# Whole fp32 products for five pieces of the second weight in the first two token groups

## The chip, the cores and the metric

The kernel runs on one core of one Trainium2 chip. The metric is the device time of one execution in microseconds (us). Three runs of the kernel before took 847.70, 844.62 and 848.91 us, median 847.7. The core's engines are named as in the profile: PE is the matrix engine (PEld its weight loads), DVE the vector engine, ACT the scalar engine, POOL the general engine and SP the engine that issues most of the transfers.

## The reference, cut to what matters

Three layers follow each other. A gated linear recurrence over 768 positions (4 batches, 8 heads, head size 48) gives 3072 rows of 384 numbers. A dense layer computes h = x @ w_in (384 to 2048), g = h * sigmoid(h), and x2 = g @ w_out (2048 to 384). A routed layer then picks one of eight experts for each row.

```python
def _moe_ref(x, w_in, w_out):
    h = x @ w_in
    g = h * (1.0 / (1.0 + np.exp(-h)))
    return (g @ w_out).astype(np.float32)
```

The change concerns only the last line, g @ w_out, for the first four chunks of 128 rows.

## The kernel before, in words

The 3072 rows are 24 chunks of 128 rows. The chunks are taken in groups: two groups of two chunks (0 and 1), then groups of three, and a last one of two. The recurrence of a chunk runs in six stages (`att0` to `att5`); the last one leaves the transposed rows of the chunk, split into two parts, in `xth` and `xtl` (`big` for group 0).

Both weights of the dense layer are cut into 16 pieces. `in_0` to `in_15` are 128 columns of w_in, `out_0` to `out_15` are 128 rows of w_out (128 x 384). A weight arrives as 64-bit floats. `load_piece` fetches a piece as raw words into one of four buffers `raw`, and `narrow` makes 32-bit floats of it on DVE with three instructions (L295, L298, L301; the first also appears as L199) in one of two buffers `cv`. `split` then makes two parts of it: ACT writes the rounded part `hi` (L226) and DVE the rest `lo` (L227). Four pieces share a pair of tiles, so `out_0_lo` in a row stands for pieces 0 to 3 and `out_1_lo` for pieces 4 to 7.

For a group g and a piece i the dense layer runs three functions. `moe_h` makes nine products on PE into `ph` (three parts of the rows by hi and lo of `in_i`), ACT takes the tanh (`se`, L501) and DVE forms the gated value (`sg`, L503). `moe_g` splits this value: ACT writes `gh` (L511), DVE writes `gl` (L512). `moe_o`, two steps later, adds three products for each chunk to `px`: gh by out_lo, gl by out_hi, gh by out_hi. They use the rounded type fp32r, in which one pass over the columns makes a product. With two chunks this makes six products of 128x384 for one pair (g, i) in groups 0 and 1.

The order of work is a list `seq` of steps (g, i). The first six steps belong to group 0, the next six to group 1, then the two groups take turns until piece 15, and group 2 follows at step 32. Tables (`UI`, `UO`, `ST0` to `ST6`) say in which step a piece is loaded and a stage of the recurrence is run. PE keeps the order in which the program is written. For DVE, ACT and the transfer queue of SP the framework chooses an order when the kernel is built, by its own estimate of times; only a few instructions are pinned. On the chip every engine then works through its list in order and waits at the first instruction whose input is missing.

Plain fp32 products already exist in this kernel: `pl` of chunks 0 to 6 multiplies the constant triangle by the plain values `f` (128 x 384). A plain product shows in the trace as two MATMUL records.

The eight transfers `xs<-big` (776 KB each) fill a table in memory with zeros. Each waits for a small POOL instruction that reads the `lo` part of one of the pieces 12 to 15, so that it starts only when that piece has been split, and POOL also waits for the transfer before.

Of the kernel before, what the change touches and what calls it, by code (L numbers as in the profile page):

```python
# [9 lines left out]
F32 = mybir.dt.float32  # L10
# [3 lines left out]
U32 = mybir.dt.uint32  # L14
I64 = mybir.dt.int64
# [6 lines left out]
P = 128  # L22
CAP = 512
ROW = 388
# [32 lines left out]
SG = 2  # L57
SE = 2
GB = 3
# [22 lines left out]
LMIN = -43.9  # L82
GROW = math.exp(20.0 - LMIN)
PLAIN = 7
ST = ST0, ST1, ST2, ST3, ST4, ST5, ST6
FAR = float(1 << 20)
HEAD = 2
# [6 lines left out]
def kernel(  # L94
# [14 lines left out]
    nc = tc.nc  # L109
    B, H, S, D = q.shape  # L110
    NT, DM = out.shape
    DFF = moe_w_in.shape[1]
    E, _, F2 = moe2_w1.shape
# [7 lines left out]
    GT = CPG * P  # L121
# [14 lines left out]
    raw = main.enter_context(tc.tile_pool(name="raw", bufs=4))  # L136
    phase = ExitStack()
    att = phase.enter_context(tc.tile_pool(name="att", bufs=1))
    late = phase.enter_context(tc.tile_pool(name="late", bufs=1))

    def bank(kind, name):
        return ps.tile([P, 512], F32, tag=kind, name=name, bufs={"h": 2, "x": 3, "a": 3}[kind])
# [25 lines left out]
    def use(n, i, name):  # L168
        return bank(BANKS.get(n, "aaaaaaaa")[i], name)
# [28 lines left out]
    def keep(fn):  # L198
        return lambda *a, **k: tc.keep_in_program_order(fn(*a, **k))  # L199

    def new_unit(key):
        kind = key[0]
        full = [P, 4, KC, P] if kind in ("in", "w1") else [P, 4, DM]
        nm = "_".join(str(x) for x in key)
        units[key] = tuple(wts.tile(full, F32R, tag="wt", name=f"{nm}_{x}") for x in ("hi", "lo"))

    def part_of(src, kind, i, n):
        cols = slice(i * P, (i + n) * P)
        return (src[:, cols] if kind in ("in", "w1") else src[cols, :]).rearrange("(c p) f -> p c f", p=P)
# [14 lines left out]
    def split(key, h, x, lo_engine):  # L224
        hi, lo = units[key]
        (keep(nc.scalar.copy) if key == ("w1", 1, 1) and RT > 1 else nc.scalar.copy)(hi[:, h], x)  # L226
        lo_engine.tensor_sub(lo[:, h], x, hi[:, h].bitcast(F32))  # L227

    def load_piece(kind, i):
        u, h = divmod(i, 4)  # L230
        src = moe_w_in if kind == "in" else moe_w_out
        nm = f"{kind}_{i}"
        if h == 0:
            new_unit((kind, u))
        shape = [P, KC, P] if kind == "in" else [P, 1, DM]
        if src.dtype == I64:
            t = raw.tile(shape + [2], U32, tag="raw", name=f"{nm}_raw")
            made = len(pieces_made)
            pieces_made.append(i)
            load_raw(t.rearrange("p c f w -> p c (f w)"), src, kind, i, nc.scalar if made < RAW else nc.sync)  # L240
            x = raw.tile([P, ROW], U32, tag="cv", name=f"{nm}_cv", bufs=2)[:, :DM].rearrange("p (c f) -> p c f", c=shape[1])
            t2 = t.rearrange("p c f w -> p (c f) w")
            pin = keep if i < (PI if kind == "in" else PO) else lambda fn: fn
            narrow(t2, x.rearrange("p c f -> p (c f)"), pin)
            x = x.bitcast(F32)
        else:
            x = raw.tile(shape, F32, tag="raw", name=f"{nm}_raw")
            nc.sync.dma_start(out=x, in_=part_of(src, kind, i, 1))
        split((kind, u), h, x if kind == "in" else x[:, 0], nc.vector)

    def verify_piece(kind, i, s):
        src = moe_w_in if kind == "in" else moe_w_out
# [59 lines left out]
    def att0(n):  # L312
        f = loaded.pop(("f", n))
        g, _ = group_of[n]
        if g < 2 or n == starts[g]:
# [3 lines left out]
            nc.scalar.activation(t, t, AF.Ln, bias=1.0)  # L319
        if n < PLAIN:  # L320
            lf[n] = (f.rearrange("p h d -> p (h d)"),)
# [19 lines left out]
    def att1(n):  # L341
        pl = use(n, 0, f"pl_{n}")
        if n < PLAIN:
            pe.matmul(pl[:, :DM], tri, lf.pop(n)[0], start=True, stop=True)
# [142 lines left out]
    gt = {}  # L487
    ht = {}

    def moe_h(g, i):  # L490
        GT = sizes[g] * P
        xh, xl = (x[:, : sizes[g]] for x in xt[g])
        wh, wl = units["in", i // 4]
        ph = bank("h", f"ph_{g}_{i}")
        m = i % 4
        for c in range(KC):
            pe.matmul(ph[:, :GT], wh[:, m, c, :], xl[:, :, c, :], start=c == 0, stop=False)
            pe.matmul(ph[:, :GT], wl[:, m, c, :], xh[:, :, c, :], start=False, stop=False)
            pe.matmul(ph[:, :GT], wh[:, m, c, :], xh[:, :, c, :], start=False, stop=c == KC - 1)
        e = att.tile([P, GT], F32, tag="se", name=f"se_{g}_{i}", bufs=SE)  # L500
        nc.scalar.activation(e, ph[:, :GT], AF.Tanh, scale=0.5)  # L501
        t = att.tile([P, GT], F32, tag="sg", name=f"sg_{g}_{i}", bufs=SG)
        nc.vector.scalar_tensor_tensor(out=t, in0=e, scalar=1.0, in1=ph[:, :GT], op0=ALU.add, op1=ALU.mult)  # L503
        ht[g, i] = t

    def moe_g(g, i):
        GT = sizes[g] * P
        t = ht.pop((g, i))
        hi = att.tile([P, GT], F32R, tag="gh", name=f"gh_{g}_{i}", bufs=GB)
        lo = att.tile([P, GT], F32R, tag="gl", name=f"gl_{g}_{i}", bufs=GB)  # L510
        (nc.scalar.copy if g < GACT else nc.vector.tensor_copy)(hi, t)  # L511
        (nc.gpsimd if (g, i) < LOV else nc.vector).tensor_sub(lo, t, hi.bitcast(F32))  # L512
        gt[g, i] = (hi, lo)

    def moe_o(g, i):
        hi, lo = gt.pop((g, i))
        first, last = (0,), (NF - 1,)
        wh, wl = units["out", i // 4]
        if i in first:
            px[g] = [bank("a" if (g, t) == (1, 1) else "x", f"px_{g}_{t}") for t in range(sizes[g])]  # L520
        for t in range(sizes[g]):
            o = px[g][t][:, :DM]
            m = slice(t * P, (t + 1) * P)
            pe.matmul(o, hi[:, m], wl[:, i % 4, :], start=i in first, stop=False)
            pe.matmul(o, lo[:, m], wh[:, i % 4, :], start=False, stop=False)
            pe.matmul(o, hi[:, m], wh[:, i % 4, :], start=False, stop=i in last)
        if i in last:
            moe_x2(g, i)

    x2 = {}  # L530
# [575 lines left out]
    def at(slot, fn, *args):  # L1106
        plan.setdefault(slot, []).append((fn, args))
# [4 lines left out]
    for n in range(NCH):  # L1112
        g, r = group_of[n]
        if n < len(ST):
            so = ST[n]
            s0 = ld = LD[n]
# [15 lines left out]
    for u in range(4):  # L1132
        for h in range(4):
            at(UI[4 * u + h], load_piece, "in", 4 * u + h)
            at(UO[4 * u + h], load_piece, "out", 4 * u + h)
    for j in range(2 * NF):
        s = VS + j * VD // 2
        at(s, verify_piece, ("in", "out")[j % 2], j // 2, s)
# [54 lines left out]
    first = min(plan)  # L1193
# [15 lines left out]
    g = NG - 1  # L1209
# [8 lines left out]
    def preload():  # L1218
        for j in range(2):
            load_expert_unit(("w1", 1, j), nc.vector)  # L1220

    todo = dict(
        o=lambda: moe_o(*outs.pop(0)), f=lambda: fill(1), F=lambda: fill(len(ops)), l=lambda: logits_pe(g),
        m=lambda: logits_pe2(g), p=lambda: pick(g), r=lambda: route(g), w=preload, k=rank_rest,
        g=rest_fetch, t=lambda: turn(items["rest"]),
# [50 lines left out]
```

## Time and profile before

| what | value |
|---|---|
| median of three runs | 847.7 us |
| profiled execution: its own time | 845.27 us |
| profiled execution: span from first to last instruction | 843.6 us |
| PE busy | 810.5 us, 96% of the span |
| DVE busy | 483.4 us, 57% |
| ACT busy | 377.1 us, 45% |
| mean granted clock of PE | 0.989 |

The shares are averages over the whole span. In the slices of 21 us that the profile shows, DVE has 9 tenths in the second to the fifth slice and 4 to 6 tenths later, so the shares of the first 110 us are not those of the whole. A wait in the lists names the instruction that waited and the one that released it.

### The profile page before, as it was taken

How to read it: one execution, taken by the hardware profiler on the slowest of the kernel's cores; microseconds unless marked ns; L12 is line 12 of the kernel's file. 1: busy time of each engine (PE TensorE's matmuls, PEld its weight loads, DVE VectorE, ACT ScalarE, POOL GpSimd, SP SyncE). 2: the span in 40 equal slices, each digit the busy share in tenths (PEclk: the TensorE clock that was granted, in tenths of full speed). 3: DMA queues.
4: the chain of work that ended last, by engine and by line, in shares of the span. 5: the costliest groups of instructions: out<-in, count | busy, mean ns of one | idle time of the engine just before them, and what ended most of it. 6: DMA issues, size and time to landing. Idle time of an engine off the chain costs nothing.

```text
span 843.6 us, 15324 instructions
## 1 busy us (share of the span) xinstructions
PE 810.5 (96%) x5692; PEld 766.8 (91%) x5692; DVE 483.4 (57%) x1293; ACT 377.1 (45%) x805; POOL 59.1 (7%) x94
## 2 busy tenths in 40 slices
PE   7799989999999999999999999999999999999994
PEld 4689889999999999999999999989999999999993
DVE  5999965566665556555666556366464526435520
ACT  4565464453453453444444333365273525435520
POOL 2000000002001001001001000001110010110001
PEclk9899999999999999999999999999999999999998
DMA  9856863313244343254343321342281615624500
GB/s 206 189 147 163 250 193 96 66 39 101 74 100 104 74 94 106 67 105 104 76 95 94 86 57 48 104 132 67 97 276 55 200 56 171 200 80 164 168 16 27
DMA packets 166435, 95.92 MB, mean 114 GB/s; under 512 B 115692, under 2 KB 159965, under 8 KB 166352
## 3 DMA queue, kind: packets, MB, share of 16 engines
q1 hardware_dynamic: 162224, 83.80, 37.5%
q0 software_dynamic: 3280, 9.49, 2.9%
q10 hardware_dynamic: 848, 1.57, 0.6%
q8 instruction: 46, 0.75, 0.4%
q14 instruction: 37, 0.30, 0.1%
HBM read 75.61 MB, written 16.33 MB: 109 GB/s over the span
## 4 chain that ended last, share of the span: by engine, by line
PE 60%; DMA 12%; issue 10%; DVE 9%; ACT 4%; SPq 3%; POOLq 0%; POOL 0%; DVEq 0%; ACTq 0%
PE px L333 19%; PE ph L333 18%; DMA out_dram<-o,oi 6%; PE py L333 4%; PE po L333 4%; PE p L333 4%; PE sc L333 2%; DMA w_raw<-in_moe_w_dram 1%; DMA f<-in_f_logit_dram 1%; DVE am L404 1%; PE pl L333 1%; PE p_r L333 1%; PE po_r L333 1%; PE pq L338 1%; PE pk L338 1%
## 5 line engine op out<-in xcount | busy, mean ns | idle before, releaser
L333 PE MATMUL px<-out_lo,gh 128*128 128x384 f32 x384 | 137.3, 357 | 0.3 <-ACT gh L511 0.3
L501 ACT ACTIVATE se<-ph 128x384 f32<-128x384 f32 (+1 forms) x144 | 65.3, 454 | 159.7 <-PE ph L333 157.1
L333 PE MATMUL px<-out_hi,gl 128*128 128x384 f32 x384 | 130.2, 339 | 2.2 <-DVE gl L512 2.2
L333 PE MATMUL px<-out_hi,gh 128*128 128x384 f32 x384 | 129.7, 338 | 0.0
L333 PE MATMUL ph<-xtl,in_hi 128*128 128x384 f32 (+1 forms) x384 | 125.5, 327 | 1.2 <-DVE sg L503 0.9
L503 DVE SCALAR_TENSOR_TENSOR sg<-se,ph 128x384 f32<-128x384 f32 (+1 forms) x144 | 73.0, 507 | 90.9 <-ACT se L501 89.0
L333 PE MATMUL ph<-xth,in_hi 128*128 128x384 f32 (+1 forms) x384 | 124.0, 323 | 0.0
L333 PE MATMUL ph<-xth,in_lo 128*128 128x384 f32 (+1 forms) x384 | 123.8, 322 | 0.0
L511 ACT CAST gh<-sg 128x384 fp32r<-128x384 f32 (+1 forms) x144 | 68.7, 477 | 70.5 <-DVE sg L503 61.5
L512 DVE TENSOR_TENSOR gl<-sg,gh 128x384 fp32r<-128x384 f32 (+1 forms) x144 | 73.4, 510 | 29.2 <-ACT gh L511 28.1
L333 PEld LDWEIGHTS ph<-xtl,in_hi 128*128 128x128 f32 x384 | 72.5, 189 | 3.8 <-issue 1.4
L333 PEld LDWEIGHTS px<-out_hi,gl 128*128 128x128 f32 x384 | 72.6, 189 | 3.6 <-DVE gl L512 3.2
L333 PEld LDWEIGHTS px<-out_lo,gh 128*128 128x128 f32 x384 | 72.4, 188 | 3.2 <-ACT gh L511 0.9
L333 PEld LDWEIGHTS ph<-xth,in_lo 128*128 128x128 f32 x384 | 72.5, 189 | 0.0
L333 PEld LDWEIGHTS ph<-xth,in_hi 128*128 128x128 f32 x384 | 72.4, 189 | 0.0
L333 PEld LDWEIGHTS px<-out_hi,gh 128*128 128x128 f32 x384 | 72.3, 188 | 0.0
L227 DVE TENSOR_TENSOR w_lo<-w_raw,w_hi 128x384 fp32r<-128x384 f32 x128 | 65.1, 552 | 12.5 <-ACT w_hi L226 11.8
L333 PE MATMUL po<-w_lo,hh 128*128 128x384 f32 (+6 forms) x200 | 67.8, 339 | 0.0
L333 PE MATMUL po<-w_hi,hh 128*128 128x384 f32 (+6 forms) x200 | 67.2, 336 | 0.0
L333 PE MATMUL po<-w_hi,hl 128*128 128x384 f32 (+6 forms) x200 | 67.2, 336 | 0.0
L226 ACT CAST w_hi<-w_raw 128x384 fp32r<-128x384 f32 x124 | 56.9, 513 | 22.8 <-DMA w_raw<-in_moe_w_dram 19.5
L333 PE MATMUL p<-xsl,w_hi 128*128 128x480 f32 (+6 forms) x168 | 58.5, 348 | 0.0
(243 smaller groups left out, 1437.9 us busy)
## 6 DMA issues: line engine op xcount, KB each, us to landing
w_raw<-in_moe_w_dram SPq DMA_DIRECT2D x64, 384.0 KB
xs<-big SPq DMA_DIRECT2D x8, 776.0 KB
out_again<-in_moe_w_out_dram SPq DMA_DIRECT2D x16, 384.0 KB
xe<-xs SPq DMA_DIRECT2D x7, 776.0 KB
out_raw<-in_moe_w_out_dram SPq DMA_DIRECT2D x13, 384.0 KB
f<-in_f_logit_dram SPq DMA_DIRECT2D x24, 192.0 KB
k<-in_k_dram SPq DMA_DIRECT2D x24, 192.0 KB
q<-in_q_dram SPq DMA_DIRECT2D x24, 192.0 KB
```

The lines of the kernel that those rows point to most:

```text
L226: (keep(nc.scalar.copy) if key == ("w1", 1, 1) and RT > 1 else nc.scalar.copy)(hi[:, h], x)
L227: lo_engine.tensor_sub(lo[:, h], x, hi[:, h].bitcast(F32))
L333: ins = nc.tensor.matmul(*a, **k)
L338: ins = nc.tensor.transpose(*a, **k)
L404: nc.vector.tensor_tensor(out=a, in0=sc4, in1=tri4, op=ALU.mult)
L501: nc.scalar.activation(e, ph[:, :GT], AF.Tanh, scale=0.5)
L503: nc.vector.scalar_tensor_tensor(out=t, in0=e, scalar=1.0, in1=ph[:, :GT], op0=ALU.add, op1=ALU.mult)
L511: (nc.scalar.copy if g < GACT else nc.vector.tensor_copy)(hi, t)
L512: (nc.gpsimd if (g, i) < LOV else nc.vector).tensor_sub(lo, t, hi.bitcast(F32))
```

## The change

Pieces 0 to 4 of w_out are no longer split when they are loaded. `narrow` writes them into a tile of their own (`out_0_x` to `out_4_x`, in the five buffers that later hold the rows `x2`). For groups 0 and 1 the gated value of these pieces stays one plain tile (`sgp`, in a buffer of `gh`), and one plain fp32 product for each chunk takes the place of three. The split into hi and lo, which groups 2 and later use, is asked for in steps 28 to 33.

```diff
+SPL = 28, 29, 30, 31, 33
...
+            if whole(kind, i):
+                x = whole_home(i)
+            else:
+                x = raw.tile([P, ROW], U32, tag="cv", name=f"{nm}_cv", bufs=2)
...
+        if whole(kind, i):
+            wholes[i] = x[:, 0]
+        else:
+            split((kind, u), h, x if kind == "in" else x[:, 0], nc.vector)
...
+    def whole(kind, i):
+        return kind == "out" and i < len(SPL) and moe_w_out.dtype == I64
...
+    def whole_home(i):
+        return att.tile([P, ROW], U32, tag="x2", name=f"out_{i}_x", bufs=5)
...
+    def split_late(i):
+        u, h = divmod(i, 4)
+        split(("out", u), h, wholes.pop(i), nc.vector)
...
+        if g < 2 and whole("out", i):
+            t = att.tile([P, GT], F32, tag="gh", name=f"sgp_{g}_{i}", bufs=GB)
...
     def moe_g(g, i):
...
+        if g < 2 and whole("out", i):
+            gt[g, i] = t, None
+            return
...
+            if lo is None:
+                pe.matmul(o, hi[:, m], wholes[i], start=i in first, stop=i in last)
+                continue
...
+    for i, s in enumerate(SPL):
+        if whole("out", i):
+            at(s, split_late, i)
```

On PE nothing else moves: at ten places six products become two. DVE's list is rebuilt. The first place is DVE between the state update of chunk 0 and the last part of the rows of chunk 1 (`big<-pt_1`), which the first product of the dense layer needs. The last rows of this place in the kernel before:

```order
L462 TENSOR_TENSOR state_85<-pu_1_395,state_85 48x4x48 x2
L227 TENSOR_TENSOR out_0_lo_214<-out_2_cv_278,out_0_hi_213 128x384
L463 TENSOR_TENSOR state_85<-state_85,a_all_84 48x4x48 x2
L227 TENSOR_TENSOR in_0_lo_266<-in_1_cv_316,in_0_hi_265 128x384
L199 TENSOR_SCALAR out_3_cv_324<-out_3_raw_322 128x384
L199 TENSOR_SCALAR in_2_cv_351<-in_2_raw_348 128x384
L298 SCALAR_TENSOR_TENSOR out_3_cv_324<-out_3_raw_322,out_3_cv_324 128x384
L482 TENSOR_TENSOR big_91<-pt_1_461,big_91 128x384
```

The same place in the changed kernel:

```order
L228 TENSOR_TENSOR in_0_lo_262<-in_1_cv_310,in_0_hi_261 128x384
L200 TENSOR_SCALAR out_3_x_318<-out_3_raw_316 128x384
L482 TENSOR_TENSOR state_85<-pu_1_387,state_85 48x4x48 x2
L228 TENSOR_TENSOR in_0_lo_262<-in_2_cv_343,in_0_hi_261 128x384
L318 SCALAR_TENSOR_TENSOR out_3_x_318<-out_3_raw_316,out_3_x_318 128x384
L483 TENSOR_TENSOR state_85<-state_85,a_all_84 48x4x48 x2
L200 TENSOR_SCALAR in_4_cv_413<-in_4_raw_410 128x384
L321 SCALAR_TENSOR_TENSOR out_3_x_318<-out_3_raw_316,out_3_x_318 128x384
L502 TENSOR_TENSOR big_91<-pt_1_453,big_91 128x384
```

The splits of the pieces `out` are gone from here, and passes over pieces that stood behind `big<-pt_1` (all of `in_2`, the first of `in_4`, the last of `out_3`) now stand ahead of it.

The second place is DVE behind the masked scores of chunk 5 (`am_5_0`, `am_5_1`), up to the inputs of chunk 6 (`kpad0<-en_6`). In the kernel before it begins with these rows:

```order
L404 TENSOR_TENSOR am_5_1_1265<-sc_5_1_1254,trir_78 128x512
L298 SCALAR_TENSOR_TENSOR out_11_cv_1156<-out_11_raw_1154,out_11_cv_1156 128x384
L512 TENSOR_TENSOR gl_0_8_1293<-sg_0_8_1251,gh_0_8_1292 128x256
L295 TENSOR_SCALAR in_13_cv_1189<-in_13_raw_1186 128x384
L301 SCALAR_TENSOR_TENSOR out_11_cv_1156<-out_11_raw_1154,out_11_cv_1156 128x384
L298 SCALAR_TENSOR_TENSOR in_13_cv_1189<-in_13_raw_1186,in_13_cv_1189 128x384
L301 SCALAR_TENSOR_TENSOR in_13_cv_1189<-in_13_raw_1186,in_13_cv_1189 128x384
L227 TENSOR_TENSOR out_2_lo_895<-out_11_cv_1156,out_2_hi_894 128x384
L295 TENSOR_SCALAR out_12_cv_1223<-out_12_raw_1221 128x384
```

In the changed kernel it begins with these:

```order
L424 TENSOR_TENSOR am_5_1_1175<-sc_5_1_1164,trir_78 128x512
L538 TENSOR_TENSOR gl_0_8_1203<-sg_0_8_1161,gh_0_8_1202 128x256
L321 SCALAR_TENSOR_TENSOR in_14_cv_1196<-in_14_raw_1193,in_14_cv_1196 128x384
L228 TENSOR_TENSOR out_3_lo_1130<-out_12_cv_1133,out_3_hi_1129 128x384
L228 TENSOR_TENSOR out_0_lo_214<-out_0_x_217,out_0_hi_213 128x384
L228 TENSOR_TENSOR out_0_lo_214<-out_1_x_240,out_0_hi_213 128x384
L228 TENSOR_TENSOR out_0_lo_214<-out_2_x_274,out_0_hi_213 128x384
L228 TENSOR_TENSOR out_0_lo_214<-out_3_x_318,out_0_hi_213 128x384
L315 TENSOR_SCALAR out_13_cv_1239<-out_13_raw_1237 128x384
```

The pieces out_11, in_13 and nearly all of out_12 and in_14 are now ahead of am_5, and four of the five late splits have been placed behind it by the framework, well before the steps that the table names. The split of the fifth, out_4, stays early, between pieces 7 of `in` and 6 of `out`.

The third place is the transfer queue of SP, where the last pieces, the zero fill and the inputs `f` of chunks 7 to 9 meet. Before:

```order
L219 DMA out_15_raw_1482<-in_moe_w_out_dram 128x768
L1172 DMA xs_76<-big_91 128x4x388
L193 DMA f_7_1621<-in_f_logit_dram 128x8x48 x3
L358 DMA ends_75<-ep_6_1318 1x384
L193 DMA k_7_1627<-in_k_dram 128x8x48
L193 DMA q_7_1625<-in_q_dram 128x8x48
L1172 DMA xs_76<-big_91 128x4x388
```

Now:

```order
L220 DMA out_15_raw_1392<-in_moe_w_out_dram 128x768
L1204 DMA xs_76<-big_91 128x4x388
L194 DMA v_6_1031<-in_v_dram 128x8x48
L1204 DMA xs_76<-big_91 128x4x388
L194 DMA f_7_1531<-in_f_logit_dram 128x8x48 x2
L378 DMA ends_75<-ep_6_1228 1x384
L194 DMA f_7_1531<-in_f_logit_dram 128x8x48
```

The third zero fill now stands ahead of `f_7`, which waited behind two of them before.

## Rows read from the trace of the kernel before

**Rows 1.** Busy time of the engines in four stretches, with PE's clock and DMA share.

```profile
core 0: us, PE busy (x) PEld busy (x) DVE busy (x) ACT busy (x) POOL busy (x), PEclk, DMA share, GB/s
27.20:44.70 17.50, 14.71 (x121) 13.03 (x121) 15.87 (x37) 13.07 (x24) 0.00 (x0) 0.81 0.90 198
44.70:91.00 46.30, 44.68 (x369) 42.39 (x367) 44.58 (x111) 25.83 (x63) 0.00 (x0) 1.00 0.60 155
91.00:107.00 16.00, 12.73 (x83) 11.83 (x79) 15.86 (x38) 6.70 (x18) 0.69 (x3) 0.89 0.92 271
...
120.00:500.00 380.00, 378.53 (x2877) 362.28 (x2875) 223.07 (x619) 167.20 (x334) 16.54 (x19) 1.00 0.36 88
```

**Rows 2.** What PE waited for in the first 180 us: total, times, longest.

```profile
PE py L333 <- DVE state L460: 2.1, 1, 2.1
PE ph L333 <- DVE big L482: 1.5, 1, 1.5
```

**Rows 3.** Chain of work that ended last: start, duration to the next piece, what.

```profile
28.06 1.03 PE pq L338 x4
...
75.52 0.65 PE pl L333 x2
76.16 1.05 PE px L333 x6
...
80.72 0.44 PE pq L338 x4
```

**Rows 4.** PE in order of time: start, duration, instruction, [idle before and releaser].

```profile
32.71 0.39 PE L333 MATMUL ph<-big,in_hi 128*128 128x256 f32 x1 [1.52 <-DVE big L482]
...
47.28 0.39 PE L333 MATMUL ph<-big,in_hi 128*128 128x256 f32 x1 [1.03 <-ACT in_hi L226]
...
47.92 0.39 PE L333 MATMUL ph<-big,in_lo 128*128 128x256 f32 x1 [0.26 <-DVE in_lo L227]
...
89.96 1.16 PE L333 MATMUL sc<-qt,kt 48*128 48x128 f32 x16
```

**Rows 5.** DVE in order of time, 23 to 33 us.

```profile
23.43 0.74 DVE L460 TENSOR_TENSOR state<-pu,a_all 48x192 f32<-48x192 f32 x2
...
31.51 0.55 DVE L298 SCALAR_TENSOR_TENSOR out_cv<-out_raw,out_cv 128x384 uint32<-128x384 uint32 x1
32.09 0.56 DVE L482 TENSOR_TENSOR big<-pt,big 128x384 fp32r<-128x384 f32 x1
```

**Rows 6.** DVE in order of time, 91 to 109 us.

```profile
91.62 1.28 DVE L404 TENSOR_TENSOR am<-sc,trir 128x512 f32<-128x512 f32 x2
92.81 0.55 DVE L298 SCALAR_TENSOR_TENSOR out_cv<-out_raw,out_cv 128x384 uint32<-128x384 uint32 x1
93.28 0.42 DVE L512 TENSOR_TENSOR gl<-sg,gh 128x256 fp32r<-128x256 f32 x1
93.62 0.35 DVE L295 TENSOR_SCALAR in_cv<-in_raw 128x384 uint32<-128x384 uint32 x1
93.89 0.55 DVE L301 SCALAR_TENSOR_TENSOR out_cv<-out_raw,out_cv 128x384 uint32<-128x384 uint32 x1
...
103.63 0.55 DVE L354 SCALAR_TENSOR_TENSOR kpad<-en,k 128x384 f32<-128x384 f32 x1
...
108.11 0.75 DVE L317 TENSOR_SCALAR f<-f 128x1152 f32<-128x1152 f32 x1
```

**Rows 7.** SP's transfer queue and POOL in order of time, 100 to 106 us.

```profile
100.04 0.40 SPq L1172 DMA_DIRECT2D xs<-big  x1
100.53 4.86 SPq L193 DMA_DIRECT2D f<-in_f_logit_dram  x3
...
105.87 0.19 POOL L1170 TENSOR_TENSOR big<-in_lo 128x1 fp32r<-128x1 f32 x1 [5.86 <-DMA xs<-big]
```

**Rows 8.** ACT in order of time, 110 to 113 us.

```profile
110.68 0.38 ACT L501 ACTIVATE se<-ph 128x256 f32<-128x256 f32 x1
111.07 1.28 ACT L319 ACT_TABLE_LOAD   x1
```

More of the change, by code (lines that the diff above doesn't have):

```diff
@@ L240, in load_piece @@
             load_raw(t.rearrange("p c f w -> p c (f w)"), src, kind, i, nc.scalar if made < RAW else nc.sync)
-            x = raw.tile([P, ROW], U32, tag="cv", name=f"{nm}_cv", bufs=2)[:, :DM].rearrange("p (c f) -> p c f", c=shape[1])
+            if whole(kind, i):
+                x = whole_home(i)
+            else:
+                x = raw.tile([P, ROW], U32, tag="cv", name=f"{nm}_cv", bufs=2)
+            x = x[:, :DM].rearrange("p (c f) -> p c f", c=shape[1])
             t2 = t.rearrange("p c f w -> p (c f) w")
@@ L248, in load_piece @@
             nc.sync.dma_start(out=x, in_=part_of(src, kind, i, 1))
-        split((kind, u), h, x if kind == "in" else x[:, 0], nc.vector)
+        if whole(kind, i):
+            wholes[i] = x[:, 0]
+        else:
+            split((kind, u), h, x if kind == "in" else x[:, 0], nc.vector)
+    wholes = {}
+    def whole(kind, i):
[5 more added lines that the diff above has]
+        split(("out", u), h, wholes.pop(i), nc.vector)
     def verify_piece(kind, i, s):
@@ L501, in moe_h @@
         nc.scalar.activation(e, ph[:, :GT], AF.Tanh, scale=0.5)
-        t = att.tile([P, GT], F32, tag="sg", name=f"sg_{g}_{i}", bufs=SG)
+        if g < 2 and whole("out", i):
+            t = att.tile([P, GT], F32, tag="gh", name=f"sgp_{g}_{i}", bufs=GB)
+        else:
+            t = att.tile([P, GT], F32, tag="sg", name=f"sg_{g}_{i}", bufs=SG)
         nc.vector.scalar_tensor_tensor(out=t, in0=e, scalar=1.0, in1=ph[:, :GT], op0=ALU.add, op1=ALU.mult)
```

## The prediction

> **What bounds the kernel now.** I read four views, in this order. The table of busy time by stretch comes first, because the page's shares are means over very different stages. From 120 us on PE is busy 378.5 of 380 us [rows 1]: whatever delay or gain exists when the kernel gets there is carried to the end unchanged, so the whole question lies in the first 117 us. Up to there DVE is as full as PE: 15.9 of 17.5 us, 44.6 of 46.3 us and 15.9 of 16.0 us in the three stretches from 27 to 107 us [rows 1]. In the middle one PE is full too (44.7 of 46.3), in the other two it is not. The list of PE's waits then says for whom: almost always DVE, 2.1 us for the first state update, 1.5 us for the second part of `big` [rows 2]; a wait of 1.03 us for piece in_3 [rows 4] goes through ACT, which itself waited for DVE's passes. The chain of waits gives what one step costs on the path, and the clock: PE was granted 0.81 and 0.89 of full speed in the first and third stretch [rows 1], that is, parts of them ran at the lower of its two levels (1.2 instead of 2.4 GHz) after PE had idled; four transposes took 1.03 us there and 0.44 us later [rows 3]. The order of time on DVE, SP and ACT comes last, to place the moved work.
>
> **The change part by part.**
>
> *The products.* Six fp32r products of one pair (g, i) hold PE for 1.05 us; one plain product of the same shape, `pl`, holds it for 0.65 us at full clock [rows 3]. Two of them make 1.30 us, so each of the ten pairs costs 0.25 us more on PE. Two pairs (pieces 0 and 1 of group 0) come before 52 us, where PE waits anyway, and are counted below. The other eight fall between 52 and 82 us, where PE has hardly a gap: 8 x 0.25 = **+2.0 us** on the path. The shape and type are those of `pl`, so I give this 0.2 us either way.
>
> The Trainium skill (Perfetto Trace Analysis, Engine Utilization) says that the matrix engine's output rate is halved for FP32_LOW_HIGH. Read as half of the fp32r rate for the whole product, a pair would take 2 x 0.35 = 0.70 us and this term would be 8 x (-0.35) = -2.8 us. The trace disagrees: the plain product `pl` holds PE for 0.65 us, not 0.35 [rows 3].
>
> *The removed halves of the gated values.* Ten casts on ACT go, and ten `gl` on DVE at 0.34 us from one start to the next [rows 6]: 3.4 us of DVE. They lie between 38 and 83 us. There PE is full, so by itself this buys nothing at once; it is DVE's list that gets shorter.
>
> *The moved splits.* Each is 0.47 us on DVE (a pass over 384 columns with two inputs, from one start to the next, as 92.81 to 93.28; the cast with one input takes 0.27, as 93.62 to 93.89) [rows 6]. By the order, out_4 is still split early, and pieces 0 to 3 now stand behind `am_5`, near 95 us. So DVE gains 4 x 0.47 = 1.9 us before 35 us and pays the same 1.9 us back at 95 us.
>
> *Up to 52 us.* DVE's freed time is filled by passes over other pieces. From the state update of chunk 0 to `big<-pt_1` it took 32.09 - 23.43 = 8.66 us [rows 5]. The new list between them has thirteen passes at 0.47, three casts at 0.27, two further pairs of state instructions at 0.77 and the first pair itself: 6.1 + 0.8 + 1.5 + 0.8 = 9.2 us. The start of the state itself I find unchanged: two `lo` passes are gone ahead of it and one `lo`, two casts and a wait for ACT have come. So the first dense product, at 32.71 us before [rows 4], comes **0.6 us later**. Then the narrowing of out_4 stands ahead of `am_2`, and its transfer can't be issued before in_5's, at about 34 us. DMA is 0.90 busy here at 198 GB/s [rows 1]; two pieces of 0.39 MB take 4 us at that rate, so out_4 lands near 37 us while DVE asks for it near 35.6: a wait of 1.4 us, bounds 0 and 3. Against this, in_3 is made earlier in the list than before, and PE's wait of 1.03 + 0.26 us for it [rows 4] goes. The two pairs add 0.5 us. Sum with the wait of 1.4: 0.6 + 0.9 (what the wait leaves over at `am_2`) + 0.5 - 1.3 = +0.7; without it -0.2. A second way of counting, by the bank that `ph_0_4` waits for, gives -0.1 and -1.4, since PE also had small gaps there. I take **-0.5**, with bounds -2.0 and +1.5.
>
> *At 91 us.* The scores of chunk 5 were ready at 89.96 + 1.16 = 91.12 us [rows 4] and DVE took them up at 91.62 [rows 6], 0.5 us late. Up to here DVE's list is 3.4 us shorter, and 1.9 more for the moved splits, PE's path only some 1.5 us longer, so DVE is there first and takes them up at once: **-0.5**; bound 0 if DVE is late for other reasons.
>
> *From 91 to 107 us.* From `am_5` to the inputs of chunk 6 DVE took 103.63 - 91.62 = 12.0 us without a gap [rows 6], and PE waited for them. The new list there has the two `am` (92.81 - 91.62 = 1.2 us), sixteen passes at 0.47, the four late splits among them, four casts at 0.27 and two gated steps at 0.34: 1.2 + 7.5 + 1.1 + 0.7 = 10.5 us. **-1.5**; bounds -2.5 and 0 (if a piece isn't there in time, DMA being 0.92 busy [rows 1]).
>
> *The f of chunks 7 to 9.* In SP's queue a third zero fill stands ahead of `f_7`. POOL lets a fill start only when the one before has landed, 5.8 us after its issue (100.04 to 105.87) [rows 7]. The second fill hangs on the split of out_12, which is now near 96 us, not 99; so the third can go out near 102.4 and f_7 behind it, where before f_7 went out at 100.53 and took 4.86 us to issue [rows 7]. DVE gets f near 108.5 instead of 108.11 [rows 6]. ACT's list has also changed: `se` of step (0, 10) stood before the two table loads (1.28 us each) at 110.68 [rows 8] and now stands behind them. It comes near 114.9, PE's next dense product then starts 1.3 us later than before, but the wait of 0.9 us that followed it is gone, and PE arrives here 0.5 us or so earlier. I take **+0.1**; bounds -1 and +5.9 (the second rival).
>
> **Sum**: +2.0 - 0.5 - 0.5 - 1.5 + 0.1 = -0.4 us. The profiled execution took 845.27 us and lies 2.43 us below the median of 847.7, inside the runs' own spread. -0.4 gives 844.9 for it and **847.3** against the median.
>
> **The rivals.**
>
> *DVE was the bound, and the relief counts in full (faster).* For it: DVE is 90 to 100% busy from 27 to 107 us and is named in nearly every wait of PE. If the waits for state, `big` and in_3 (2.1 + 1.5 + 1.3 = 4.9) [rows 2, 4] vanish and one of the slow stretches with them (the clock of 0.81 over 17.5 us means 6.6 us at half speed, 3.3 us lost in two stretches, so 1.7), and the two terms behind `am_5` stand (-2.0): -8.6 + 2.5 = -6.1, **841.6**. Against it: the new list puts more, not less, ahead of the state and of `big`, and between 52 and 91 us PE is full itself.
>
> *The third zero fill holds f_7 back (slower).* If the second fill still leaves at 100.04 us, since out_15 stands ahead of it in SP's queue or in_14 is late, then the third leaves at 105.9, f_7 is issued until 111.2 and lands near 114, 5.9 us after DVE wanted it. Behind it in order stand the gated values on DVE and, on ACT, exp, two table loads and `se`; PE has no other work for that long. 5.9 in place of 0.1 makes the sum +5.4, **853.1**. It decides from the point where f reaches DVE later than about 110 us. Against it: out_12 is split three microseconds earlier by the order.
>
> *A plain product costs one record, not two.* Then the products give -2.8 instead of +2.0: **842.5**. The two records of each `pl` speak against it.
>
> That the change doesn't do what it says holds in part: the framework has put the late splits near 95 us instead of behind 105 us, and left out_4 early. This is in the sum.
>
> **How the numbers follow.** The forecast has 0.73 of the chance, with its own range 844 to 850 from the bounds of the terms up to 107 us. The first rival has 0.13, the second 0.12, the third 0.02. A measurement of this kernel tells about 0.5%, 4.2 us, from no change. The first and the third lie beyond that on the fast side; of the forecast's own spread hardly anything does. The second lies just beyond it on the slow side: I put 0.10 there. So faster 0.15, same 0.75, slower 0.10. The range that leaves about 2 in 10 out is 842.5 to 851.
>
> **What would show it.** In the changed kernel `px<-out_x` should have two records per product and the pair 1.30 us between its neighbours; anything near 0.70 or above 1.5 breaks the first term. The first `ph` should start near 33.3 us, and the wait for in_3 should be gone; DVE should show a wait for a transfer at out_4's first pass. The scores of chunk 5 should be taken up between 91.5 and 94 us, `kpad` of chunk 6 some 10.5 us behind `am_5`, and the f of chunk 7 on DVE between 107.5 and 110. From 120 us on the two traces should run in parallel. A fast clock through the first stretch, or an f later than 110, would make the prediction wrong.

## The result and the profile after

The changed kernel took 854.51, 860.64, 853.50 and 853.42 us, median 854.0; the kernel before took 846.59 us (median) beside it. The ratio is 1.0095, 95% interval 1.0068 to 1.0123: slower by some 8 us, outside the range of 842.5 to 851. The likeliest case of the prediction didn't come. The place of the loss is that of its second rival, "the third zero fill holds f_7 back" (853.1), for a reason that the rival did not give.

The profiled execution took 854.51 us, with a span of 852.8 us against 843.6. Busy time by stretch, columns as in [rows 1], with one stretch more:

```profile
27.20:44.70 17.50, 15.68 (x102) 13.14 (x101) 15.87 (x37) 6.85 (x14) 0.00 (x0) 0.61 0.94 217
44.70:91.00 46.30, 44.45 (x341) 37.15 (x340) 41.32 (x102) 25.05 (x54) 0.19 (x1) 1.00 0.65 166
91.00:107.00 16.00, 14.50 (x101) 13.83 (x101) 15.93 (x38) 8.60 (x22) 4.20 (x1) 0.89 0.58 181
107.00:120.00 13.00, 8.71 (x61) 8.14 (x60) 6.53 (x16) 4.96 (x11) 2.06 (x2) 0.94 0.86 214
120.00:500.00 380.00, 378.62 (x2857) 362.53 (x2857) 224.00 (x622) 170.36 (x338) 17.16 (x20) 0.99 0.36 88
```

From 120 us on PE is as full as before (378.62 of 380), so the loss lies ahead of it, as the prediction said it would. Two places are new. In the fourth row PE is busy for only 8.71 of 13 us and DVE for 6.53: both stood. The same stretch of the kernel before:

```profile
107.00:120.00 13.00, 12.14 (x94) 11.44 (x94) 8.73 (x20) 9.73 (x17) 0.39 (x2) 1.00 0.59 180
```

In the third row POOL, which had one instruction there, was busy for 4.20 us with it.

PE's waits, to be laid beside [rows 2]:

```profile
PE ph L353 <- DVE sg L526: 3.6, 1, 3.6
...
PE py L353 <- DVE state L480: 2.1, 1, 2.1
...
PE ph L353 <- DVE big L502: 0.9, 1, 0.9
```

A wait of 3.6 us for a gated value (`sg`) has come. Where it is from can be read in the order of time over four engines. These are the rows that answer to [rows 6] and [rows 7]:

```profile
97.85 1.29 DVE L424 TENSOR_TENSOR am<-sc,trir 128x512 f32<-128x512 f32 x2
...
99.85 0.56 DVE L228 TENSOR_TENSOR out_lo<-out_cv,out_hi 128x384 fp32r<-128x384 f32 x1
100.32 1.97 DVE L228 TENSOR_TENSOR out_lo<-out_x,out_hi 128x384 fp32r<-128x384 f32 x4
100.55 4.20 POOL L1202 TENSOR_TENSOR big<-out_lo 128x1 fp32r<-128x1 f32 x1 [10.36 <-DVE out_lo L228]
...
104.77 0.39 SPq L1204 DMA_DIRECT2D xs<-big  x1
...
108.54 0.55 DVE L374 SCALAR_TENSOR_TENSOR kpad<-en,k 128x384 f32<-128x384 f32 x1
109.02 1.86 POOL L1202 TENSOR_TENSOR big<-in_lo 128x1 fp32r<-128x1 f32 x1 [4.28 <-DMA xs<-big]
...
110.91 0.38 SPq L1204 DMA_DIRECT2D xs<-big  x1
111.39 1.74 SPq L194 DMA_DIRECT2D f<-in_f_logit_dram  x2
...
118.00 0.76 DVE L337 TENSOR_SCALAR f<-f 128x1152 f32<-128x1152 f32 x1 [5.56 <-DMA f<-in_f_logit_dram]
...
119.14 0.58 PE L353 MATMUL ph<-xtl,in_hi 128*128 128x256 f32 x1 [3.63 <-DVE sg L526]
```

Read from the top: out_12 is split at 99.85 and the four late splits follow. POOL's one-column instruction, the gate of the second zero fill, starts at 100.55 and ends at 104.75; the same kind of instruction took 0.19 us in [rows 7]. The second fill leaves at 104.77. The third gate takes 1.86 us, the third fill leaves at 110.91, and `f_7`, behind it in SP's queue, at 111.39, where it left at 100.53 before [rows 7]. DVE has nothing ahead of `f_7` left to do and waits 5.56 us, the gated step behind it waits with DVE, and PE waits 3.63 us for that step.

Not all of the 9.2 us between the two profiled executions belongs to the change. A second profile of the kernel before (run e5 below, 849.95 us) and a second one of the changed kernel (e4, 855.34 us) have the same start (the scores of chunk 1 at 21.77 and 21.75 us), so they can be laid side by side. PE in the kernel before:

```profile
21.77 1.16 PE L333 MATMUL sc<-qt,kt 48*128 48x128 f32 x16
...
34.78 0.48 PE L333 MATMUL ph<-big,in_hi 128*128 128x256 f32 x1 [0.46 <-DVE big L482]
...
63.78 0.39 PE L333 MATMUL ph<-xtl,in_hi 128*128 128x256 f32 x1 [0.29 <-DVE xtl L482]
...
92.60 1.16 PE L333 MATMUL sc<-qt,kt 48*128 48x128 f32 x16
...
114.43 1.16 PE L333 MATMUL sc<-qt,kt 48*128 48x128 f32 x16
```

and in the changed kernel:

```profile
21.75 1.16 PE L353 MATMUL sc<-qt,kt 48*128 48x128 f32 x16
...
35.92 0.38 PE L353 MATMUL ph<-big,in_hi 128*128 128x256 f32 x1 [0.93 <-DVE big L502]
...
65.37 0.38 PE L353 MATMUL ph<-xtl,in_hi 128*128 128x256 f32 x1 [0.70 <-DVE xtl L502]
...
95.59 1.16 PE L353 MATMUL sc<-qt,kt 48*128 48x128 f32 x16
...
118.77 0.38 PE L353 MATMUL ph<-xtl,in_hi 128*128 128x256 f32 x1 [2.92 <-DVE sg L526]
120.02 1.33 PE L353 MATMUL sc<-qt,kt 48*128 48x128 f32 x10
```

| place on PE | later than before by | of it in this stretch | forecast for the stretch |
|---|---|---|---|
| scores of chunk 1 | 0.0 us | | 0 |
| first dense product | 1.1 | +1.1 | +0.6 |
| first product of group 1 | 1.6 | +0.5 | -0.6 |
| scores of chunk 5 | 3.0 | +1.4 | +1.5 |
| scores of chunk 6 | 5.6 | +2.6 | -1.9 |
| end of the span (848.2, 853.6) | 5.4 | -0.2 | 0 |

The last column lays the terms of the prediction on these stretches (-0.6 is the rest of -0.5 and two pairs of products, +1.5 six pairs, -1.9 the three terms from 91 us on). The last stretch but one holds more than half of the miss: 4.5 us of 5.8.

### The profile page after: what moved, and what is told of

The parts are those of the page before. It is cut to its first block, busy times and chain, and to the rows that moved or that the text cites. A ratio compares the mean times of both kernels' runs of the same rounds, so it can differ in the third digit from the quotient of the medians.

```text
span 852.8 us, 15260 instructions
## 1 busy us (share of the span) xinstructions
PE 819.3 (96%) x5672; PEld 769.0 (90%) x5672; DVE 480.0 (56%) x1283; ACT 373.2 (44%) x795; POOL 65.2 (8%) x94
## 4 chain that ended last, share of the span: by engine, by line
PE 51%; DMA 19%; issue 14%; DVE 9%; ACT 3%; SPq 2%; POOL 1%; POOLq 0%; DVEq 0%; ACTq 0%
PE ph L353 19%; PE px L353 19%; DMA out_dram<-o,oi 10%; PE py L353 4%; PE sc L353 2%; DMA f<-in_f_logit_dram 2%; DVE w_lo L228 2%; DMA out_dram<-o_r,oi_r 1%; DMA w_raw<-in_moe_w_dram 1%; PE pl L353 1%; DVE sg L526 1%; DMA in_again<-in_moe_w_in_dram 1%; PE pk L358 1%; PE plt L358 1%; DMA out_again<-in_moe_w_out_dram 1%
## 5 line engine op out<-in xcount | busy, mean ns | idle before, releaser
L353 PE MATMUL ph<-xtl,in_hi 128*128 128x384 f32 (+1 forms) x384 | 127.7, 332 | 4.8 <-DVE sg L526 3.6
L353 PE MATMUL px<-out_lo,gh 128*128 128x384 f32 x364 | 129.8, 357 | 0.0
L353 PE MATMUL px<-out_hi,gl 128*128 128x384 f32 x364 | 123.6, 340 | 2.7 <-DVE gl L538 2.7
L353 PE MATMUL px<-out_hi,gh 128*128 128x384 f32 x364 | 123.0, 338 | 0.0
L526 DVE SCALAR_TENSOR_TENSOR sg<-se,ph 128x384 f32<-128x384 f32 (+1 forms) x134 | 68.9, 514 | 89.7 <-ACT se L521 89.3
L537 ACT CAST gh<-sg 128x384 fp32r<-128x384 f32 (+1 forms) x134 | 64.6, 482 | 67.4 <-DVE sg L526 61.7
L538 DVE TENSOR_TENSOR gl<-sg,gh 128x384 fp32r<-128x384 f32 (+1 forms) x134 | 69.3, 518 | 29.7 <-ACT gh L537 29.2
L353 PEld LDWEIGHTS px<-out_hi,gl 128*128 128x128 f32 x364 | 69.1, 190 | 3.5 <-DVE gl L538 3.4
L353 PEld LDWEIGHTS px<-out_lo,gh 128*128 128x128 f32 x364 | 68.9, 189 | 2.3 <-issue 0.4
L353 PEld LDWEIGHTS px<-out_hi,gh 128*128 128x128 f32 x364 | 68.8, 189 | 0.0
```

What stands on the lines that cost most here:

```text
L353: ins = nc.tensor.matmul(*a, **k)
```

## The experiments

Each run's ratio is to the kernel before, run beside it on the same chip. f_7 stands for the f of chunks 7 to 9.

**e4, the changed kernel again, and e5, the kernel before again** (no edit).

> The changed kernel itself once more, for a second profile and more times. In the first profile PE ran at half speed from 10.7 to 18 us, where the profile of the kernel before was at full speed from 11 us, with the same work in front of it; that is 2.6 us of the difference of 9.2 between the two profiled executions. If that is chance of one execution, profiles of both kernels and of these variants show now the one, now the other start, and times fall in groups 2 to 3 us apart. If the change causes it, every variant with the five pieces narrowed into their own tiles shows pl_1 at 1.65 us and the first masked scores at 18.1 us.

> The kernel before itself, for a second profile. In its first profile (845.27 us) PE reached full speed at 11 us, the first masked scores came at 15.5 us and the first dense product at 32.7 us; in all five profiles of the changed kernel and its variants PE ran at half speed up to 16 to 18 us and the first dense product came between 35.9 and 38.1 us. If the change causes the slow start and the long slow stretch behind 29 us, this profile looks like the first one: pl_1 near 0.9 us, first dense product near 32.7 us. If both are chance or the chip's, it looks like those of the changed kernel: pl_1 1.65 us, first dense product 35 us or later, a time of 847 to 850 us.

e4: 856.22 us median, ratio 1.0099 (1.0079 to 1.0119), the first result again. e5: one execution, 849.95 us. Both have `pl` of chunk 1 at 1.65 us, as every profile of this study but the first one of the kernel before (0.91 us): the slow start is not the change's, and the first comparison of profiles overstated the loss by some 2.6 us. The first dense product came at 34.78 us in e5, between the two cases that were expected.

**e1, f_7 ahead of the third fill.** SP's order is pinned; the lists of DVE, ACT and POOL are the same.

```
+ pin = keep if nm == "f" and n in (7, 8, 9) else lambda fn: fn
- nc.sync.dma_start(out=t, ...)
+ pin(nc.sync.dma_start)(out=t, ...)
...
- nc.sync.dma_start(out=xs[...], in_=zrow...)
+ (keep(nc.sync.dma_start) if i >= 2 else nc.sync.dma_start)(out=xs[...], in_=zrow...)
```

> The changed kernel with one difference: in SP's queue the f of chunks 7 to 9 stand ahead of the third zero fill, behind two fills as in the kernel before. DVE's, ACT's and POOL's lists are the same. Theory A (the third fill holds f_7 back): the second fill still leaves near 104.8 us, f_7 is issued from about 105.7 us instead of 111.4 and reaches DVE near 113 instead of 118.0; DVE's wait of 5.56 us for it falls below 1 us, PE's wait of 3.63 us falls by at least 3, and the slow clock of 1.3 us behind it goes: 4 to 5 us less than the changed kernel, about 849.5. Rival B (the loss was there before f_7 came: slow start, longer products, longer early lists; the late f only fills time that PE would wait anyway): f_7 comes earlier, the time stays within 1 us of 854.

851.36 us median, ratio 1.0044 (1.0025 to 1.0062), against 1.0099 for e4 on the same chip: 0.0055 x 849 = 4.7 us back. The rows in order of time:

```profile
100.45 4.20 POOL L1203 TENSOR_TENSOR big<-out_lo 128x1 fp32r<-128x1 f32 x1 [10.36 <-DVE out_lo L229]
104.67 0.40 SPq L1205 DMA_DIRECT2D xs<-big  x1
...
105.95 2.71 SPq L201 DMA_DIRECT2D f<-in_f_logit_dram  x2
...
112.76 0.76 DVE L338 TENSOR_SCALAR f<-f 128x1152 f32<-128x1152 f32 x1 [0.43 <-DMA f<-in_f_logit_dram]
```

The gate still takes 4.20 us, but f_7 leaves at 105.95, DVE waits 0.43 us for it, and the scores of chunk 6 come 20.57 us behind those of chunk 5 (95.83 to 116.40), against 24.4 in e4 and 21.8 in e5. The 4 to 5 us that were expected came as a difference; the time itself, expected near 849.5, did not, and the kernel before took 848.88 beside it and not 846.59. Rival B is out for these 4.7 us; theory A has to be narrowed by e6 below.

**e2, the second gate on ACT.** DVE's and SP's lists are the same.

```
+ x = lo[:, PW[i]].bitcast(F32)
+ if i == 1:
+     nc.scalar.mul(spare, x, 0.0)
+ else:
+     tc.keep_in_program_order(nc.gpsimd.tensor_sub(spare, x, x))
```

> The changed kernel with one difference: the small instruction that lets the second zero fill start (it reads the lo part of out_12 and writes one column of the row of zeros) runs on ACT instead of POOL. The lists of DVE and SP are the same. Theory C (POOL's instruction took 4.20 us instead of 0.19 because DVE's back-to-back passes kept POOL from the memory): on ACT it takes under 0.3 us near 100.6, the second fill leaves near 101 us instead of 104.8, lands near 105; the third gate, still on POOL, starts near 105 and ends when DVE next reads from PSUM (near 107.9), so the third fill leaves near 108 and f_7 near 108.5 instead of 111.4: 2.5 to 3.5 us less than the changed kernel, about 851. Rival D (the second fill was late because what it waits for was late): the second fill leaves near 104.8 again and the time stays within 1 us of 854.

853.55 us median, ratio 1.0051 (1.0033 to 1.0070), some 4 us less than e4.

```profile
101.53 1.28 DVE L424 TENSOR_TENSOR am<-sc,trir 128x512 f32<-128x512 f32 x2
...
104.17 0.20 ACT L1203 ACTIVATE big<-out_lo 128x1 fp32r<-128x1 f32 x1
104.40 0.39 SPq L1206 DMA_DIRECT2D xs<-big  x1
```

This execution was 3.7 us late ahead of these rows, so distances count: the second fill left 2.9 us behind `am_5`, against 6.9 (97.85 to 104.77) with the gate on POOL. What the gate waits for was ready; POOL could not work. The fill then took 5.75 us to its next gate (104.40 to 110.15) instead of 4.25, so f_7 left only at 110.86, 9.3 us behind `am_5` instead of 13.5. DVE's wait for it fell from 5.56 to 1.45 us. Theory C holds as to the second gate: on POOL it is slow, on ACT it isn't. The third gate, which was expected to be held again, took 0.20 us here.

**e9 and e10, DVE takes up f_7 later**, in the changed kernel and in the kernel before. SP's queue keeps its order around the fills and f_7, and POOL's list is the same.

```
- nc.vector.tensor_scalar_max(t, t, FMIN)
+ (keep if n == 7 else lambda fn: fn)(nc.vector.tensor_scalar_max)(t, t, FMIN)
```

> The changed kernel with one difference: DVE takes up the f of chunks 7 to 9 some ten gated steps later in its list (ACT's two passes and two table loads for it follow). Third fill ahead of f_7, POOL's gate and the four splits in a row stay, so POOL's second gate should again take near 4.2 us and f_7 be issued 5 us later than in the first run of the series. If the loss is only that DVE stands waiting for f with a gated step of PE behind it, the wait of 5.5 us and PE's wait of 2.9 to 3.6 us vanish although f is as late as before: from the scores of chunk 5 to those of chunk 6 near 20 us instead of 24.4 to 25.4, and 4 to 6 us less than the changed kernel, a ratio near 1.003 to the kernel before. If the late transfer itself costs (chunk 7 is late), the ratio stays near 1.0099.

> The kernel before with the same single pin: DVE takes up f_7 later. In it DVE waits for f_7 only 0.3 us and nothing stands behind it, so by the theory of the wait the gain is small: the table loads on ACT no longer stand ahead of a gated step (from the scores of chunk 5 to those of chunk 6 about 20 us instead of 21.8): 1 to 2 us faster, ratio 0.998. If chunk 7 comes late by it: slower. If faster it is a version that beats both.

e9: 853.10 us median, ratio 1.0044 (1.0026 to 1.0062). In e9 all that made f_7 late is still there:

```profile
101.55 4.21 POOL L1202 TENSOR_TENSOR big<-out_lo 128x1 fp32r<-128x1 f32 x1 [10.36 <-DVE out_lo L228]
...
110.41 0.38 SPq L1204 DMA_DIRECT2D xs<-big  x1
110.89 1.74 SPq L194 DMA_DIRECT2D f<-in_f_logit_dram  x2
...
137.35 0.75 DVE L200 TENSOR_SCALAR f<-f 128x1152 f32<-128x1152 f32 x1
```

DVE comes to f_7 at 137.35 us, long after it has landed, and nothing waits. The distance between the scores of chunk 5 and 6 was 22.8 us, not the 20 expected (PE's granted clock was 0.50 from 100 to 108 us), yet the ratio is that of e1. A late f_7 costs nothing by itself; DVE standing in front of it with a gated step behind does.

e10: 848.14 us median, ratio 0.9990 (0.9973 to 1.0008). The distance from the scores of chunk 5 to those of chunk 6, expected near 20 us, is 21.8 (92.84 to 114.65), the same as in e5. Only further on is something gained in its profile: the transposes of chunk 6 come 33.9 us behind the scores of chunk 5 (92.84 to 126.70) against 35.7 in e5 (92.60 to 128.28). The times can't tell that from no change.

**e6, the kernel before with the third fill ahead of f_7.** The pins of e1, and the fills one step earlier (`PF = 21`).

> The kernel before with one edit: the third zero fill stands ahead of the f of chunks 7 to 9 in SP's queue, as in the changed kernel (the framework has moved DVE's first pass over f behind two gated steps in answer). Theory A (a third fill ahead of f_7 is by itself the loss of 4 to 5 us): the third fill leaves near 106 us, f_7 reaches DVE near 113 instead of 108, and the kernel is 2 to 5 us slower than before. Rival (the fill matters only together with POOL's gate held for 4.2 us, which the changed kernel's four splits in a row caused): the third fill leaves 4 us earlier in this kernel than it does there, f_7 is late by little, and the time is within 1.5 us of the kernel before.

848.30 us median, ratio 0.9988 (0.9975 to 1.0002). Theory A as it was put here is wrong. f_7 was as late as in the changed kernel:

```profile
109.07 0.39 SPq L200 DMA_DIRECT2D xs<-big  x1
109.55 0.46 SPq L200 DMA_DIRECT2D f<-in_f_logit_dram  x1
...
117.71 0.76 DVE L318 TENSOR_SCALAR f<-f 128x1152 f32<-128x1152 f32 x1 [4.49 <-DMA f<-in_f_logit_dram]
```

DVE even waits 4.49 us. But the framework, which knew of the later transfer, had put the pass over f_7 behind two more gated steps, so PE had work and lost 0.89 us. This and e9 say the same: what costs is a list made for an early f_7 that meets a late one.

**e8, f_7 later on DVE and all late splits behind it**, on top of e1. The pins of e1 and e9, and `keep` on the subtraction in `split_late`.

> The first run of this series with two more pins: DVE takes up the f of chunks 7 to 9 where the program has it (behind step 13 of the groups, some 12 us later), and all five late splits behind that. Theory A says the loss at f_7 is a wait of DVE with gated steps behind it: with f late in DVE's list nothing waits for its transfer, PE's wait of 0.9 us behind it goes, and the late splits no longer stand between the scores and the inputs of chunk 6 (1.9 us of DVE, of which PE feels at most 0.7): 1 to 2 us less than the first run, near 850. POOL's second gate takes under 1 us, since four passes in a row are gone. Rival: f so late makes chunk 7 late itself (its first product is due near 136 us), and the time rises by 1 us or more.

850.58 us median, ratio 1.0019 (1.0002 to 1.0037). With the four passes gone from behind out_12 the gate is short again:

```profile
99.59 0.31 POOL L1206 TENSOR_TENSOR big<-out_lo 128x1 fp32r<-128x1 f32 x1 [10.43 <-DVE out_lo L229]
```

Ahead of it now runs a pass of DVE with one input. The executions spread from 847.2 to 854.2 us; the profiled one (847.20 us, span 845.5) is the shortest. The median is still 1.5 us above that of the kernel before (849.09), about the price of the products (below).

**e3, plain products with the splits at load**, and **e7, two whole pieces instead of five**, both with the pins of e1.

```
e3: - else:
    + if True:
          split((kind, u), h, ...)
    ... (split_late is never called)
e7: - SPL = 28, 29, 30, 31, 33
    + SPL = 28, 29
```

> The changed kernel with the five pieces split as soon as they are narrowed (as in the kernel before) and kept whole besides, so that the plain products stay and no split moves; f_7 stands behind two fills as in the first run of this series. It stands against the kernel before by the products and the missing casts alone. If the plain products cost what their rows show (0.25 us for each of eight pairs) and the moved splits cost nothing of their own: +2 against the kernel before, near 848.5, and within 1 us of the first run of this series. If the moved splits and the list rebuilt around them (four splits in one row behind the scores of chunk 5, the gate held by them) are the larger cost: the same +2, and the first run of this series 2 us or more above it. If the missing casts relieve DVE: at or below 846.6.

> The first run of this series (f of chunks 7 to 9 ahead of the third fill) with two whole pieces instead of five: four pairs of plain products instead of ten, of which two in group 1 lie where PE is full (+0.5 us instead of +2.0), and both late splits are placed near 32 us. If the plain products are what is left of the loss (3.7 us against the kernel before), the time falls to 1 us above the kernel before, near 849.5 on this scale. If the list rebuilt ahead of the first dense product is, it stays at 851 or rises, since the two splits now stand ahead of the second part of the rows of chunk 1.

e3: 851.69 us median, ratio 1.0037 (1.0024 to 1.0050), the same as e1: taken together, what the moved splits give early and cost late comes to nothing, once f_7 stands ahead of the third fill. That each of the two is nothing is not shown; in its profile e3 is later than e1 at the first product of group 1 (by 2.7 us, counted from the scores of chunk 1) and still ends only 0.7 us later (851.71 and 851.05). e7: 854.37 us, ratio 1.0069 (1.0054 to 1.0084), slower than with five pieces. Why is not shown. Its two late splits stand ahead of the second part of `big`, and PE waits 2.17 us for that (0.91 in e1), but the first dense product still comes earlier behind the scores of chunk 1 than in e1 (22.81 to 36.01, 13.2 us; 22.45 to 36.67, 14.2). The first product of group 1 is late (47.6 us behind them, 43.2 in e1), and the granted clock was 0.50 from 38 to 54 us; the profiled execution (851.28 us) is the shortest of six. Both runs price the products. From the first product of group 1 to the scores of chunk 5, where PE hardly waits, the kernel before took 28.8 us in both of its profiles, and in e6 and e10 (61.16 to 89.96 in the first, 63.78 to 92.60 in e5), and the kernels with five pieces took 30.2 in all seven without added products (65.37 to 95.59 in e4, 67.69 to 97.91 in e3). Six pairs lie there: 1.4 / 6 = 0.23 us for each. e7 has two there and took 29.26 (70.43 to 99.69): 0.22 each.

**e11 and e12, fifteen products of ones more** between 25 and 38 us, in e8 and in the kernel before.

```
+ for s in (-4, -4, -4, -1, -1):
+     at(s, keep_warm)
```

> The eighth run (f of chunk 7 late on DVE, late splits behind it) with fifteen more products of ones by ones on PE, nine in the wait of 2.1 us ahead of the first product with the state of chunk 1 and six ahead of the first dense product. Theory E (in the changed kernel the granted clock stays at half for 12 to 20 us behind 29 us because PE waits in that stretch, and which of the two it is makes the times fall in groups 4 us apart): with PE busy there the clock is full from 30 us on in more of the stretch, the group of 853 to 854 us vanishes, median near 847.5. If the clock there follows something else: the same groups, or 1 us slower for the added products.

> The kernel before with the same fifteen products. Its clock was at half for some 14 us between 28 and 50 us in its second profile. If the clock theory holds it gains too, 1 to 2 us, and less than the changed kernel's upper group; if nothing changes in the clock there, it is 0 to 1 us slower.

e11: 850.49 us, ratio 1.0019 (1.0003 to 1.0035), as e8. e12: 849.66 us, ratio 1.0004 (0.9988 to 1.0021). Not conclusive on the clock: in e11 it was full from 27 to 32 us and 0.59 from 32 to 40 (0.50 in e8), but the first dense product came later (38.44 us), since six of the added products took 2.2 us on the path. From the scores of chunk 1 to the first product of group 1 e11 then took 41.6 us (22.94 to 64.55; 42.7 in e8, 42.0 in e5), but e12 took 46.4 (22.97 to 69.37), with a wait of 3.36 us for a piece of the first weight and the clock at 0.50 from 52 to 60 us. So the kernel before, with the added products, can be late here by over 4 us too, and the medians show no gain from them.

No version of these is faster than the kernel before by more than can be told.

## Why the prediction was wrong, step by step

- **The products** (+2.0): right. 0.23 us for each pair measured, 0.25 forecast, and each product has its two records.
- **Up to 52 us** (-0.5, bounds -2.0 and +1.5): the direction of its parts was right (the wait for in_3 is gone, of which e5 has only 0.26 us; the first dense product is later), the size wrong. That product is 1.1 us late instead of 0.6, and PE waits for `xtl` of group 1 0.4 to 0.9 us more. At the first product of group 1 the kernel is 1.6 us late in e4, not 0.0. Counted from the scores of chunk 1 (42.0 us in e5) it was 0.7 to 1.6 late in four profiles with five whole pieces (the first one, e1, e4, e8) and 3.0 to 4.8 in e9, e3 and e2. DVE's announced wait of 1.4 us for out_4 is 0.39 us in e4 and not there in the first profile. A wait that the sum did not have came ahead of the first dense product. In e4:

```profile
25.23 0.73 DVE L480 TENSOR_TENSOR state<-pu,a_all 48x192 f32<-48x192 f32 x2
...
29.43 0.36 DVE L200 TENSOR_SCALAR in_cv<-in_raw 128x384 uint32<-128x384 uint32 x1 [0.42 <-DMA in_raw<-in_moe_w_in_dram]
...
35.31 0.56 DVE L502 TENSOR_TENSOR big<-pt,big 128x384 fp32r<-128x384 f32 x1
```

By the order of the list this is in_2, whose first pass stood just ahead of `big<-pt_1` before and now stands some 6 us ahead of it, where the piece has not landed. The list took 10.1 us (25.23 to 35.31) and not the 9.2 that were counted; 0.42 of it is this wait. The wait is there in all eight profiles with five whole pieces, from 0.35 us to 1.99 (e11), and in no profile of the kernel before. In e2 and e9 it is 1.76 and 1.56 us, 1.34 and 1.14 more than in e4, and the first dense product comes later by just that (15.51 and 15.30 us behind the scores of chunk 1, 14.17 in e4).
- **At 91 us** (-0.5): wrong. In the first profile of the changed kernel DVE takes the scores up 1.92 us after PE starts them (95.93 to 97.85), 0.26 later than before. A shorter list did not mean that DVE was there first.
- **From 91 to 107 us** (-1.5): right. `kpad_6` came 10.7 us behind `am_5` (97.85 to 108.54), 10.5 forecast, 12.0 before.
- **The f of chunks 7 to 9** (+0.1): this is the step that failed. It said that the second fill follows the split of out_12 and that "the third can go out near 102.4 and f_7 behind it". The split did come earlier, 2.0 us behind `am_5` instead of 7.4. But the step took the gate as free, by its 0.19 us in [rows 7], and did not ask what DVE would run beside it. The four late splits were put right behind that split, the gate took 4.20 us and the next one 1.86, so the third fill left at 110.91 and f_7 reached DVE at 118.00, with DVE and then PE waiting for it. Had both taken 0.3, the third fill would have left near 105.4 (100.55 + 0.3 + 4.25 + 0.3) and f_7 near 105.9, as in e1: the third fill alone would have cost nothing. That is worked out, not run.
- **The second rival** named the place, the wait of DVE and PE for f_7 and nearly its price (5.9 us for 4.7 measured), and got a chance of 0.12. Its reason for the late fill was another: out_15 ahead of it in SP's queue, or in_14 late, where the fill waited for POOL's gate. So its time (853.1) came near in part by luck. Its point of decision (f later than 110 us) isn't one: f reached DVE at 112.76 in e1 and at 117.71 in e6, and DVE's place in its list decided. It was weighed by "out_12 is split earlier", which was true and beside the point.
- **The base**: the sum was made against a profile of 845.27 us whose start was the only one of fourteen with `pl` of chunk 1 at 0.91 us.

In sum: 4.7 us by e1 at f_7; 1.9 us for eight pairs of products; 1 us or more ahead of group 1; and -1.3 us behind `am_5`. That makes 6.3 of the 8.4 us (0.0099 x 849) by which e4 is slower; the rest is not assigned. What stays open is the size of the part ahead of group 1. PE waited there, and its granted clock was then 0.50 for some 12 us in e1 and e8 but up to 52 us in e2 and e3, with the same lists of work in e1 and e2 up to there. The executions of e2 fall in two groups (850.25 to 850.93 and 853.08 to 857.47); that the clock in this stretch divides them is not shown, since one execution of each run was profiled. The times of the kernel before (845.61 to 852.23 in 35 runs on the last chip) show no such gap, though e12 was as late there. e11 did not settle why.

## What to carry to other kernels

Where a built order places a pass over a transfer's data ahead of work that the bound engine needs, ask what happens if the transfer is 5 us late, and follow the transfer's own gates back through every engine; an instruction that took 0.2 us took 4.2 when its neighbours changed. Put the pass behind that work, or the transfer ahead of bulk fills: e1 and e9 each gave back some 4.7 us (0.0055 x 849) by pinning the order of a few instructions. Take a second profile of the old kernel before working out sums of 1 or 2 us.

## What the runs showed of the hardware

POOL's gate reads and writes one column of 128 values. The second gate took 4.20, 4.20, 4.20 and 4.21 us in the four profiles in which it started beside the four passes of DVE with two inputs from the on-chip memory (the changed kernel's two, e1, e9), and 0.30 or 0.31 in all nine others with the gate on POOL, where it started beside a pass with one input (the first instruction of `narrow`). On ACT (e2) it took 0.20 us beside the same four passes. Once held, POOL did not get in at the next change of instruction: ten passes of DVE began or ran in the 4.20 us, two of them with one input, and each began before the one ahead of it had ended. The first gap between two passes is at the end:

```profile
104.13 0.56 DVE L318 SCALAR_TENSOR_TENSOR in_cv<-in_raw,in_cv 128x384 uint32<-128x384 uint32 x1
104.73 0.56 DVE L321 SCALAR_TENSOR_TENSOR in_cv<-in_raw,in_cv 128x384 uint32<-128x384 uint32 x1
```

DVE's two-input passes stand 0.47 us apart, these two 0.60, and the gate ended at 104.75. The gap is not POOL's doing, for in e2, where no gate waits on POOL, the same two passes stand 0.59 us apart:

```profile
107.82 0.55 DVE L318 SCALAR_TENSOR_TENSOR in_cv<-in_raw,in_cv 128x384 uint32<-128x384 uint32 x1
108.41 0.56 DVE L321 SCALAR_TENSOR_TENSOR in_cv<-in_raw,in_cv 128x384 uint32<-128x384 uint32 x1
```

That the gap let POOL in is argued and not shown. It needn't be a gap: the third gate of the first profile (109.02 to 110.88) ended 0.13 us into a pass that began at 110.75 and reads one of its two inputs from a result of PE (`sg<-se,ph`).

The Trainium skill (SBUF — State Buffer, SBUF: two separate sides) says that DVE and GpSimd share one port pair under an exclusive lock, and that a DVE operation in a 2-port mode, or one with two inputs in SBUF, holds it against a GpSimd operation that reads SBUF. The trace agrees as to the two-input passes (the gate beside them took 4.20 us, beside a one-input pass 0.30). Why the two one-input passes within the 4.20 us did not let the gate in, no run here settles. The same section of the Trainium skill also says that the lock is held "for the whole instruction"; here one POOL instruction was held over several, 4.20 us where one pass takes 0.56.
